# A retention layer with an MLP on one core: decay in q and v alone, states copied, g folded into w1, x normalized ahead of the first product

## The chip, the core and the metric

The program runs on one core of a Trainium2 chip. Five engines work beside each other, each in its own order: TensorE (PE, matmul; its weight loads are shown as PEld), VectorE (DVE), ScalarE (ACT), GpSimd (POOL) and SyncE (SP). They wait for one another by semaphores. Sixteen DMA engines move data; SP, ACT and POOL put transfers on queues. TensorE writes into eight PSUM banks of 128 x 512 float32; the other engines read the results from there. The metric is device time in microseconds.

## What is computed

For four batches and eight heads a state of 64 x 64 decays by a head's factor at each of 768 positions and takes up k times v; q reads it. The heads side by side give x of 512 columns, which goes through a normalization, two matrices with a relu between them, and a residual.

```python
gamma = 1.0 - 2.0 ** (-5.0 - np.arange(H))
for t in range(S):
    state = gamma * state + einsum('bhd,bhe->bhde', k[:, :, t], v[:, :, t])
    y[:, :, t] = scale * einsum('bhd,bhde->bhe', q[:, :, t], state)
x = y.transpose(0, 2, 1, 3).reshape(B, S, 512)
xn = (x - mean(x)) / sqrt(var(x) + 1e-6) * g_ln
out = x + maximum(xn @ w_ch1, 0) @ w_ch2          # 512 x 2048, 2048 x 512
```

Inputs and output are float32.

## The kernel before

**Tiles.** The 768 positions of a batch are six chunks of 128, so there are 24 tiles of 128 positions. `TILES` numbers the four chunks 0 first (tiles 0 to 3), then chunks 1 to 5 of batch 0 (4 to 8), of batch 1 (9 to 13) and so on. Matrices are bfloat16 on the chip, sums float32.

**A tile's attention.** q, k and v are loaded (tokens `q`, `k`, `v`; POOL issues them, and the transfer turns float32 into bfloat16). For tiles 0 to 6 (`T0` = 7) TensorE transposes q and k into PSUM (`tq`, `tk`); for later ones a DMA transpose on SP's queue does it (`tr`). `eq` multiplies the transposed q by a decay that grows from the start of the chunk, `qsc`. `vis` makes the scores of k and q, and from tile 7 on also the product of q with the state; from tile 8 on it does so for two tiles at once. `am` multiplies the scores by `mask`, which holds the causal triangle and the inverse decay of the key's position. `py` multiplies them with v. The same v times an inverse decay counted from the start of the sequence (`vg`, POOL) goes with k into the running sum of a batch, which one PSUM bank holds (`pd`, bank PD), and `pb` reads that sum into a bfloat16 state, multiplied by the decay of the chunk's start (`gch`): two VectorE instructions, one per half of the partitions, since a state holds pairs of heads and only the diagonal blocks are written; the rest was set to zero at the start.

**A tile's MLP.** `bn` takes mean and variance, `xn` subtracts the mean and multiplies by g, `xc` copies y into `x_all` for the residual. Up to tile 9 (`S0` = 10) the division by the standard deviation comes last, in the addition `ad`, since relu lets a positive factor pass; from tile 10 on ScalarE does it behind `xn` (`sr`, `rt`, `xg`), on a float32 copy. `tx` and `ex` transpose x for the first product, tiles 0 to 7 on TensorE, later ones by DMA. The first product (`m`) goes by groups of one, two or four tiles: a piece fills one bank (16, 8 or 4 matmuls of 128, 256 or 512 columns), and a relu (`r`, mostly ScalarE) empties it. The second product goes tile by tile (`z`, 16 matmuls of 512 columns), but from tile 10 on two tiles together with seven products in place of eight (`s` 1 to 7, Strassen's scheme in Winograd's form): four sums of weight blocks are made once (`tm`), four differences of blocks of relu output per pair (`sa`, VectorE), and `o` adds the products and x together. `st` stores a tile from ScalarE's queue.

**Weights.** w1 comes in four column pieces of 512 (`W0` to `W3`), w2 in four row pieces (`Z0` to `Z3`), all on POOL's queue. `gb` spreads g over the partitions by a float32 matmul. `warm` is a matmul on zeros.

**The order** is written out by hand: `ORDER` lists tokens, and each engine runs its own in that order. `m0_4//X1` is a piece of the first product into bank X1, `r0_4/A` its relu on ScalarE, `/D` means VectorE, `/S` SP, `/P` POOL. Most banks have a fixed part: X0 to X3 scores and the first product, Y0 and Y1 y, M the second product, PD the running sum. POOL's loads stand in its own order, and before a load that overwrites a buffer it waits with a one-element copy (`gate`).

## Time and profile before

| | us |
|---|---|
| three runs | 208.21, 1157.15, 210.58 |
| median | 210.58 |
| span of the profiled execution | 205.7 |

The page gives of the profiled execution its span, from the first to the last instruction, and no other time. The fastest of the three runs lies 2.5 above that span; one run was disturbed. A row such as "busy us" counts an engine's time in instructions; a matmul's own duration is longer than its distance to the next, because matmuls overlap. The chain of waits follows the work back from the last instruction. The granted TensorE clock was 0.997 over the span.

The start in order of time, by the chain: TensorE, ScalarE and VectorE have first data from 4.2 us on, the first product with w1 starts at 14.4 us. POOL issues its last load at 132.7 us; the last DMA transpose is issued at 163.5 us.

### The profile page before, as it was taken

The numbers are of one execution on the slowest core, as the hardware profiler recorded it, in microseconds if no ns is written. First come the engines' busy times: TensorE is split into PE (matmuls) and PEld (weight loads), VectorE is DVE, ScalarE is ACT, GpSimd is POOL, SyncE is SP. The second block draws the span as 40 slices with busy tenths as digits, with TensorE's granted clock in tenths as the row PEclk, the third lists the DMA queues.
The fourth block names the chain that finished last, engine by engine and source line by source line (L and its number), as shares of the span: only waits on it lengthen the run. The fifth ranks groups of instructions, "written<-read, shape, count | busy, mean of one in ns | idle before, by whom it ended". The sixth has DMA issues, their size and how long they took to land.

```text
span 205.7 us, 5388 instructions
## 1 busy us (share of the span) xinstructions
PE 198.7 (97%) x2183; PEld 147.5 (72%) x2183; DVE 156.4 (76%) x365; ACT 87.1 (42%) x191; POOL 96.5 (47%) x145
## 2 busy tenths in 40 slices
PE   7998999999999999999998999999999999999993
PEld 2568999898546568577784988987465876458882
DVE  7687889678249979979899999999868674026972
ACT  6375653650400504646263173590766504562000
POOL 8995694694498597492598077900000000000000
PEclk9999999999999999999999999999999999999998
DMA  8999999999999999999999999997010313111025
GB/s 127 166 183 178 162 191 168 174 182 153 160 110 181 140 123 137 180 92 175 171 175 154 136 247 169 164 160 138 3 51 0 81 26 149 58 51 51 0 101 208
DMA packets 109948, 27.13 MB, mean 132 GB/s; under 512 B 102626, under 2 KB 106978, under 8 KB 109923
## 3 DMA queue, kind: packets, MB, share of 16 engines
q0 software_dynamic: 77024, 13.37, 86.5%
q1 hardware_dynamic: 28242, 6.85, 25.4%
q10 hardware_dynamic: 4656, 6.56, 10.1%
q8 instruction: 17, 0.28, 0.6%
q14 instruction: 9, 0.07, 0.1%
HBM read 27.30 MB, written 6.29 MB: 163 GB/s over the span
## 4 chain that ended last, share of the span: by engine, by line
PE 81%; DVE 7%; DMA 5%; POOL 3%; issue 2%; ACT 1%; POOLq 0%; ACTq 0%
PE X L529 35%; PE M L547 12%; PE M L606 10%; PE Y L606 5%; DMA w<-in_moe_w_ch_dram 5%; PE Y L547 3%; PE X L606 3%; PE PD L606 3%; PE X L404 2%; PE Y L432 2%; DVE sum L595 2%; PE PD L474 2%; DVE asb L417 1%; POOL early L346 1%; POOL k L346 1%
## 5 line engine op out<-in xcount | busy, mean ns | idle before, releaser
L529 PE MATMUL X<-xnt,w 128*128 128x128 bf16 (+2 forms) x880 | 89.6, 255 | 0.5 <-DMA w<-in_moe_w_ch_dram 0.5
L529 PEld LDWEIGHTS <-w 128*128 128x128 bf16 x896 | 66.3, 98 | 19.4 <-DMA w<-in_moe_w_ch_dram 0.7
L540 ACT ACTIVATE h<-X 128x512 bf16<-128x512 f32 x85 | 48.5, 601 | 50.9 <-PE X L529 46.3
L417 DVE TENSOR_TENSOR asb<-X,mask 128x512 bf16<-128x512 f32 x48 | 30.5, 683 | 3.3 <-PE X L404 3.1
L547 PE MATMUL M<-w,h 128*128 128x512 bf16 x128 | 30.6, 379 | 0.0
L456 ACT CAST x_all<-Y 128x256 bf16<-128x256 f32 (+1 forms) x39 | 14.4, 408 | 28.7 <-DVE bns L440 13.1
L547 PEld LDWEIGHTS <-h 128*128 128x128 bf16 x160 | 14.9, 98 | 14.8
L466 POOL TENSOR_TENSOR vg<-v,vsc 128x512 bf16<-128x512 bf16 x19 | 20.1, 1058 | 9.9 <-DMA v<-in_v_dram 9.9
L606 PEld LDWEIGHTS <-h 128*128 128x128 bf16 x224 | 21.7, 98 | 3.5 <-issue 0.3
L346 POOL DMA_DIRECT2D v<-in_v_dram x23 | 20.8, 907 | 3.0 <-DMA w<-in_moe_w_ch_dram 2.5
L440 DVE BATCH_NORM_STATS2 bns<-Y 128x6 f32<-128x256 f32 (+1 forms) x39 | 16.1, 450 | 5.2 <-PE Y L432 4.6
L606 PEld LDWEIGHTS <-sum 128*128 128x128 bf16 x168 | 16.3, 98 | 2.8 <-issue 0.3
L484 DVE TENSOR_TENSOR state<-PD,gch 64x256 bf16<-64x256 f32 x40 | 16.6, 414 | 0.3
L346 POOL DMA_DIRECT2D qk<-in_q_dram x17 | 15.2, 895 | 1.3 <-issue 0.7
L346 POOL DMA_DIRECT2D qk<-in_k_dram x17 | 15.2, 898 | 0.9 <-issue 0.8
L620 DVE TENSOR_TENSOR osb<-M,x_all 128x256 f32<-128x256 f32 (+1 forms) x12 | 6.1, 505 | 10.5 <-PE M L606 10.4
L595 DVE TENSOR_TENSOR sum<-h,sum 128x1024 bf16<-128x1024 bf16 x14 | 10.6, 756 | 0.2
L395 DVE TENSOR_TENSOR trq<-tr,qsc 128x512 bf16<-128x512 bf16 x17 | 7.6, 454 | 3.3 <-DMA tr<-qk 3.2
L626 PE MATMUL PD<-zeros 128*128 128x512 bf16 (+1 forms) x33 | 8.9, 404 | 1.2 <-DVE zeros L259 1.2
L375 POOL COPY scrap<-qk 1x1 bf16<-1x1 bf16 x28 | 5.8, 208 | 8.1 <-DMA qk<-in_k_dram 7.2
L432 PEld LDWEIGHTS <-asb 128*128 128x128 bf16 x192 | 8.0, 98 | 2.1 <-DVE asb L417 0.4
L552 DVE SCALAR_TENSOR_TENSOR osb<-M,rstd,x_all 128x512 f32<-128x512 f32 x8 | 6.0, 750 | 3.5 <-PE M L547 3.5
(115 smaller groups left out, 256.6 us busy)
## 6 DMA issues: line engine op xcount, KB each, us to landing
out_dram<-osb ACTq DMA_DIRECT2D x23, 256.0 KB, 2.5
w<-in_moe_w_ch_dram POOLq DMA_DIRECT2D x8, 512.0 KB, 8.7
v<-in_v_dram POOLq DMA_DIRECT2D x23, 128.0 KB, 7.1
qk<-in_k_dram POOLq DMA_DIRECT2D x17, 128.0 KB, 6.0
qk<-in_q_dram POOLq DMA_DIRECT2D x17, 128.0 KB, 6.6
early<-in_q_dram POOLq DMA_DIRECT2D x6, 128.0 KB, 7.5
k<-in_k_dram POOLq DMA_DIRECT2D x3, 128.0 KB, 7.6
early<-in_k_dram POOLq DMA_DIRECT2D x3, 128.0 KB, 8.5
```

The costliest lines, as they stand in the source:

```text
L346: nc.gpsimd.dma_start(out=dst, in_=tok[kind][TILES[t]])
L417: nc.vector.tensor_tensor(out=slot(asb, t)[:, :, par, :], in0=bank(("pa", t, par)).rearrange("p (i t) -> p i t", t=P), in1=mask.rearrange( ...
L432: nc.tensor.matmul(dst, lhsT=slot(asb, t)[:, h // 2, h % 2, :], rhs=v_of(t)[:, h, :], start=(not late and n == H and h == 0), stop=(h >= H ...
L440: nc.vector.bn_stats(out=bns[:, t, i, :], in_=x)
L456: nc.scalar.copy(out=dst, in_=src)
L466: nc.gpsimd.tensor_tensor(out=slot(vgs, chunk(t)), in0=v_of(t), in1=vsc[:, c, :].unsqueeze(2).to_broadcast([P, H, D]), op=ALU.mult)
L484: nc.vector.tensor_tensor(out=slot(state, chunk(t) - 1)[o, :, o], in0=pd[o, :, o], in1=gch[o, c - 1, :].unsqueeze(2).to_broadcast([D, NPAI ...
L529: nc.tensor.matmul(bank(("mm", g, ho))[:, j * n * P:(j + 1) * n * P], lhsT=w1[:, ko, (ho + j) * P:(ho + j + 1) * P], rhs=x[:, x0:x0 + n, k ...
L540: nc.scalar.activation(out=dst, in_=src, func=AF.Relu)
L547: nc.tensor.matmul(bank(("m2", t)), lhsT=slot(h1, t // 4)[:, ho, t % 4 * P:(t % 4 + 1) * P], rhs=w2[:, ho, :], start=(ho == 0), stop=(ho = ...
L595: {"P": nc.gpsimd, "": nc.vector}[eng].tensor_tensor(out=out, in0=in0, in1=in1, op=ALU.subtract)
L606: nc.tensor.matmul(product(t, i), lhsT=left(t, i)[:, ho, :], rhs=right[i][:, ho, :], start=(ho == 0 and i in (1, 2)), stop=(ho == HK - 1), ...
```

## The change

Decay. q is multiplied by a decay counted from the start of the sequence, so there is a table `qsc` for each chunk (six; one made by ScalarE, one by VectorE, four by POOL), and v by its inverse for all tiles (`vg`, now also the right side of `py`). The mask is then the plain triangle `cm`, and a state needs no factor: `pb` is one copy of the whole bank, 17 of 20 on ScalarE.

```diff
-        nc.vector.tensor_tensor(out=slot(trq, t), in0=x, in1=qsc, op=ALU.mult)
+        nc.vector.tensor_tensor(out=slot(trq, t), in0=x, in1=qscs[TILES[t][1]], op=ALU.mult)
...
-            in1=mask.rearrange("p (i a) t -> p a i t", a=2)[:, par], op=ALU.mult)
+            in1=cm.unsqueeze(1).to_broadcast([P, NPAIR, P]), op=ALU.mult)
...
-        for o in (slice(0, D), slice(D, P)):
-            nc.vector.tensor_tensor(
-                out=slot(state, chunk(t) - 1)[o, :, o], in0=pd[o, :, o],
-                in1=gch[o, c - 1, :].unsqueeze(2).to_broadcast([D, NPAIR, D]), op=ALU.mult)
+        evacuate(eng, slot(state, chunk(t) - 1), BANK["PD"].rearrange("p (i t) -> p i t", t=P))
...
+    @on("qs")
+    def _(eng, c):
+        if c == 0:
+            nc.scalar.activation(out=qscs[c], in_=arg, func=AF.Exp, bias=ln8, scale=1.0)
+            return
+        e = nc.vector if eng == "D" else nc.gpsimd
+        e.tensor_tensor(out=qscs[c], in0=qsf, in1=gch[:, c - 1, :].unsqueeze(2).to_broadcast([P, NPAIR, P]),
+                        op=ALU.mult)
```

Tiles 4 to 6 take the state in `vis` by halves of the partitions too, in place of the whole-pair product ahead of `py`.

g. It comes as four columns of 128 (`gc`, SP), and VectorE multiplies each piece of w1 by it after it lands and before its first use (`wg`, four instructions a piece). The matmul that spread g is gone.

```diff
+    @on("wg")
+    def _(eng, j):
+        s = slice(j * DM, (j + 1) * DM)
+        for ko in range(KO):
+            nc.vector.tensor_scalar(out=w1[:, ko, s], in0=w1[:, ko, s], scalar1=gcol[:, ko:ko + 1], scalar2=None,
+                                    op0=ALU.mult)
```

Normalization. For every tile the reciprocal of the standard deviation (`sr` on ScalarE, `rt` on VectorE) and the shift (`sh`, VectorE) are made first, and `xn` then does all of it in one instruction on either engine; `xg` and the float32 copies are gone, and `ad` only adds.

```diff
+        nc.vector.scalar_tensor_tensor(out=shift[:, t:t + 1], in0=mv[:, t, 0:1], scalar=-1.0,
+                                       in1=rstd[:, t:t + 1], op0=ALU.mult, op1=ALU.mult)
...
-        dst, src, g = y_parts(t, half, slot(xns if t < S0 else xhat, t))
-        nc.vector.scalar_tensor_tensor(out=dst, in0=src, scalar=mv[:, t, 0:1], in1=g,
-                                       op0=ALU.subtract, op1=ALU.mult)
+        dst, src = y_parts(t, half, slot(xns, t))
+        if eng == "A":
+            nc.scalar.activation(out=dst, in_=src, func=AF.Identity, bias=shift[:, t:t + 1],
+                                 scale=rstd[:, t:t + 1])
+        else:
+            nc.vector.tensor_scalar(out=dst, in0=src, scalar1=mv[:, t, 0:1], scalar2=rstd[:, t:t + 1],
+                                    op0=ALU.subtract, op1=ALU.mult)
```

So the pair of tiles 8 and 9 can go through the seven products as well (eight pairs, not seven; `z` for tiles 0 to 7).

Order. `y_of` takes its two banks by the table too, so that any bank may hold anything but the running sum. The `gate` copies, the early read of w1 (`touch`) and the zeroing of states are gone. Attention begins with tiles 0, 2, 4, 1. Of 96 relus ScalarE keeps 57 (89 before); of 32 `sa` POOL takes 16; of 44 `xn` ScalarE takes 25; of 25 stores SP takes 13. Two of its lines:

```diff
-vis0//X1,X2 gb//X3 W1 am0b vg0/ am0a gl v2 warm3_2 tq1//Y1 py0//M tk1//Y0 eq1 ek1/A k3 bn0 sqt
+vis1//X1,X3 k3/P q3/P am1b/D tq4//Y1 eq4/D rt0/D vg4/P py2//Y0 pb4/A bn2/D ba2/D sh0/D W2/P ek4/A
```

POOL's first loads before; `early`, `k_`, `v_` are buffers of single tiles, `w_92` is w1, so that its pieces are rows five and eight.

```order
L346 DMA early<-in_v_dram 128x8x64
L346 DMA k_99<-in_k_dram 128x8x64
L346 DMA early<-in_q_dram 128x8x64
L346 DMA v_102<-in_v_dram 128x8x64
L365 DMA w_92<-in_moe_w_ch_dram 128x4x512
L346 DMA k_100<-in_k_dram 128x8x64
L346 DMA early<-in_q_dram 128x8x64
L365 DMA w_92<-in_moe_w_ch_dram 128x4x512
L466 TENSOR_TENSOR vg_132<-early,vsc 128x512
```

The same start of POOL after the change (`w_95` is w1):

```order
L348 DMA k_102<-in_k_dram 128x8x64
L348 DMA v_107<-in_v_dram 128x8x64
L348 DMA early<-in_q_dram 128x8x64
L348 DMA v_109<-in_v_dram 128x8x64
L367 DMA w_95<-in_moe_w_ch_dram 128x4x512
L348 DMA v_106<-in_v_dram 128x8x64
L480 TENSOR_TENSOR vg_133<-v_107,vsc 128x512
L348 DMA k_104<-in_k_dram 128x8x64
L348 DMA early<-in_q_dram 128x8x64
L480 TENSOR_TENSOR vg_135<-v_109,vsc 128x512
L367 DMA w_95<-in_moe_w_ch_dram 128x4x512
```

Five more tile loads stand ahead of what is shown, so the first piece of w1 is POOL's tenth load, not its fifth, and between it and the next come three tile loads and two products of v with the decay.

VectorE around its first work for tile 0's and 1's MLP before (`bns` statistics, `asb` masked scores, `trq` scaled q):

```order
L440 BN_STATS bns<-M 128x6
L441 BN_AGGR mv<-bns 128x2
L450 SCALAR_TENSOR_TENSOR xn_137<-M,mv,gb 128x512
L417 TENSOR_TENSOR asb_136<-X_64,mask 128x4x128
L417 TENSOR_TENSOR asb_136<-X_61,mask 128x4x128
L440 BN_STATS bns<-M 128x6
```

And after, where VectorE scales the first piece of w1 (`w_95`):

```order
L421 TENSOR_TENSOR asb_139<-Y_66,cm 128x4x128
L421 TENSOR_TENSOR asb_139<-X_64,cm 128x4x128
L451 RECIPROCAL rstd<-rstd 128x1
L455 SCALAR_TENSOR_TENSOR shift<-mv,rstd 128x1
L373 TENSOR_SCALAR w_95<-w_95,gcol 128x512 x4
L439 BN_STATS bns<-X_63 128x6
L439 BN_STATS bns<-M 128x6
L443 BN_AGGR mv<-bns 128x2
L421 TENSOR_TENSOR asb_140<-X_62,cm 128x4x128
```

The four scalings stand between the shift of tile 2 and the statistics of tile 4, and a masked score of tile 1 (the last row) comes behind them.

The third place is VectorE at the pair of tiles 14 and 15. Before, their masked scores (four `asb`) are followed by a state and statistics:

```order
L417 TENSOR_TENSOR asb_135<-X_62,mask 128x4x128
L417 TENSOR_TENSOR asb_135<-X_61,mask 128x4x128
L417 TENSOR_TENSOR asb_136<-X_64,mask 128x4x128
L417 TENSOR_TENSOR asb_136<-X_63,mask 128x4x128
L484 TENSOR_TENSOR state_95<-PD,gch 64x4x64 x2
L440 BN_STATS bns<-Y_65 128x6
```

After:

```order
L421 TENSOR_TENSOR asb_139<-M,cm 128x4x128
L421 TENSOR_TENSOR asb_139<-X_64,cm 128x4x128
L421 TENSOR_TENSOR asb_140<-X_63,cm 128x4x128
L421 TENSOR_TENSOR asb_140<-Y_66,cm 128x4x128
L399 TENSOR_TENSOR trq_131<-tr_122,qsc_82 128x512
L399 TENSOR_TENSOR trq_128<-tr_125,qsc_84 128x512
L439 BN_STATS bns<-X_61 128x6
```

The scaled q of tiles 19 and 16 (`trq`), which read what DMA transposes bring (`tr`), now stand between the masks and the statistics.

More of the change, by code (lines that the diff above doesn't have):

```diff
@@ L32 @@
 ORDER = """
-hk0b/A hk0a/S iota small pos hq0b/A hq0a/S v0 grow table touch k1 consts idn arg lmul cm q1 vsc mask
-qsc v1 hkc0/A gch hqc0a/D zero W0 warm8_1 tk0//Y0 hqc0b/A k2 ek0/A warm1_1 tq0//Y1 eq0 q2 warm1_3
-vis0//X1,X2 gb//X3 W1 am0b vg0/ am0a gl v2 warm3_2 tq1//Y1 py0//M tk1//Y0 eq1 ek1/A k3 bn0 sqt
-warm3_1 vis1//X3,X0 q3 xn0 v3 am1a xc0 warm2_3 tx0//Y0 am1b ex0/A W2 warm3_0 py1//M warm1_0 tk2//Y0
-pd0 k4 bn1 ek2/A tq2//Y1 q4 m0_0//X3 xn1 eq2 r0_0/D vis2//X1,X2 tx1//Y0 am2a am2b m0_4//X0 v4 xc1
@@ L166 @@
     rstd = sb.tile([P, NT], FP32, name="rstd")
-    touch = sb.tile([P, KO, 16], FP32, name="touch")
+    shift = sb.tile([P, NT], FP32, name="shift")
     w1 = sb.tile([P, KO, DH], BF16, name="w1")
@@ L179 @@
     q0 = [early_h[:, 4 + i] for i in range(4)]
-    v0 = [early_h[:, 11]] + [sb.tile([P, H, D], BF16, name=f"v0{i}") for i in range(1, B)]
     trk = [early_t[:, 8 + i] for i in range(3)]
@@ L185 @@
     trq = slots("trq", [P, NPAIR, P], BF16)
+    vg0 = [early_h[:, 11]] + [sb.tile([P, H, D], BF16, name=f"vg0{i}") for i in range(1, B)]
     vgs = slots("vg", [P, H, D], BF16)
@@ L308, in _ @@
                                 op0=ALU.is_ge)
-    @on("mask")
+    @on("gc")
     def _(eng):
-        nc.vector.tensor_tensor(
-            out=mask, in0=vsc[:, 0, :].unsqueeze(2).to_broadcast([P, H, P]),
-            in1=cm.unsqueeze(1).to_broadcast([P, H, P]), op=ALU.mult)
-    @on("gch")
-    def _(eng):
-        for c in range(1, C):
-            nc.scalar.activation(out=gch[:, c - 1], in_=lgq, func=AF.Exp, bias=0.0,
-                                 scale=float(P * c))
-    @on("zero")
-    def _(eng):
-        for x in state:
-            nc.vector.memset(x, 0.0)
-    @on("grow")
-    def _(eng):
-        nc.sync.dma_start(out=grow[0:1, :], in_=moe_g_ln.rearrange("(o n) -> o n", o=1))
-    @on("touch")
-    def _(eng):
-        nc.sync.dma_start(out=touch, in_=w1_v[:, :, 0:16])
-    @on("gb")
-    def _(eng):
-        nc.tensor.matmul(bank(("mm", "g")), lhsT=ones, rhs=grow[0:1, :], start=True, stop=True)
-    @on("gl")
-    def _(eng):
-        nc.scalar.copy(out=gb, in_=bank(("mm", "g")))
+        dma(eng).dma_start(out=gcol, in_=moe_g_ln.rearrange("(ko p) -> p ko", p=P))
     @on("k", "q", "v")
@@ L406, in _ @@
         for t in ts:
-            for i in range(NPAIR if t >= T0 else 0):
+            for i in range(NPAIR if TILES[t][1] else 0):
                 for par in range(2):
@@ L671, in parse @@
-        if kind == "z":
-            t, part = map(int, arg.split("_"))
-            if where:
-                at(("m2", t))
-            return EMIT[kind], (t, part)
-        if kind == "warm":
-            return EMIT[kind], tuple(map(int, arg.split("_")))
-        return EMIT[kind], (int(arg),) if arg else ()
+        kind, arg = re.fullmatch(r"([a-zA-Z]+?)(\d.*)?", name).groups(default="")
+        keys = []
+        if kind in ("hk", "hq", "hkc", "hqc"):
+            n, half = re.fullmatch(r"(\d+)([ab]?)", arg).groups()
+            args, kind = (letter[half], kind[1], int(n)), "hc" if kind.endswith("c") else "ha"
+        elif kind in ("k", "q", "v"):
+            args = (kind, int(arg))
+        elif kind in ("tk", "tq"):
+            args = (kind[1], int(arg))
+            keys = [("tp", *args)]
+        elif kind in ("xn", "xc", "am", "st"):
+            n, half = re.fullmatch(r"(\d+)([ab]?)", arg).groups()
+            args = (int(n), letter[half])
+        else:
+            args = tuple(map(int, arg.split("_"))) if arg else ()
+            if kind == "tx":
+                keys = [("tp", "x", *args)]
+            elif kind == "vis":
+                ts = visit[args[0]]
+                keys = [("pa", t, par) for t in ts for par in range(2)] + [("y", ts[0], par) for par in range(2)]
+            elif kind == "py":
+                keys = [("y", *args)]
+            elif kind == "m":
+                keys = [("mm", *args)]
+            elif kind == "s":
+                keys = [("sm" if args[1] == 1 else "sb", args[0])]
+            elif kind == "z":
+                keys = [("m2", args[0])]
```

310 lines of the change are left out of this document (133 added, 177 removed).

## The prediction

> **What bounds the kernel now.** I read the page from the top: the share of busy time, then the chain that ended last, then the busy time by stage, then the places where TensorE waits.
>
> ```profile
> span 205.7 us, 5388 instructions
> PE 198.7 (97%) x2183; PEld 147.5 (72%) x2183; DVE 156.4 (76%) x365; ACT 87.1 (42%) x191; POOL 96.5 (47%) x145
> q0 software_dynamic: 77024, 13.37, 86.5%
> PE 81%; DVE 7%; DMA 5%; POOL 3%; issue 2%; ACT 1%; POOLq 0%; ACTq 0%
> ```
>
> TensorE is busy for 97% of the span and carries 81% of the chain. It is the bound. The loads that POOL issues (queue q0) fill 86.5% of sixteen DMA engines' span, so the feed is the second tight resource. VectorE, at 76% over the whole span, is nearly full in one stage:
>
> ```profile
> core 0: us, PE busy (x) PEld busy (x) DVE busy (x) ACT busy (x) POOL busy (x), PEclk, DMA share, GB/s
> 5.00:15.00 10.00, 9.56 (x101) 5.93 (x100) 7.36 (x16) 5.36 (x12) 9.77 (x13) 1.00 1.86 175
> 15.00:25.00 10.00, 9.06 (x168) 8.51 (x166) 8.17 (x17) 5.46 (x11) 6.48 (x8) 1.00 2.11 169
> 100.00:140.00 40.00, 39.03 (x435) 33.02 (x432) 38.75 (x88) 20.50 (x46) 24.70 (x36) 1.00 1.63 172
> 140.00:206.00 66.00, 62.22 (x518) 43.13 (x516) 39.81 (x89) 23.10 (x48) 0.00 (x0) 0.99 0.22 69
> ```
>
> From 100 to 140 us VectorE works 38.75 of 40 us, yet TensorE still works 39.03: the vector backlog costs TensorE about 1 us there. After 140 us nothing but TensorE is tight. Busy time in the first 15 us misleads, because much of it is matmuls on zeros. What counts there is when real work can run:
>
> ```profile
> 14.42 1.06 PE L529 MATMUL X<-xnt,w 128*128 128x128 bf16 x16
> 16.79 1.07 PE L529 MATMUL X<-xnt,w 128*128 128x128 bf16 x16 [0.54 <-DMA w<-in_moe_w_ch_dram]
> 20.91 0.40 PE L404 MATMUL X<-trq,early 64*128 64x128 bf16 x8 [0.36 <-DVE trq L395]
> ```
>
> The first w1 product starts at 14.42, the second stands until the second piece of w1 lands, and from 20.91 on TensorE is never held for long. The chain gives the price of each piece of TensorE work as the distance from one start to the next:
>
> ```profile
> 7.47 9.27 DMA w<-in_moe_w_ch_dram
> 18.09 0.89 PE X L529 x16
> 33.47 0.22 PE Y L426 x4
> 73.67 0.55 PE X L404 x16
> 74.22 0.23 PE Y L410 x16
> 82.47 1.73 PE M L547 x8
> 163.95 0.87 PE M L606 x8
> 202.25 0.42 DVE osb L620
> ```
>
> So a group of w1 products is 0.89, four z products (1.73 / 2) are 0.86, eight Strassen products 0.87, a set of four 128-column products 0.22, a single tile's scores 0.28 (half of 0.55), its state products 0.12. Counting the order table with these (and 0.5 for the product that spreads g), the kernel before holds 186.2 us of TensorE work. Before 20.91 it has done 8.3 of it: 12 sets at 0.22, three scores at 0.28, three y at 0.23, g, four w1 groups at 0.89. The start therefore loses 20.91 - 8.3 = 12.6 us. From 20.91 to 202.25 there are 181.3 us for 177.9 of work: 3.4 us of small waits. Then 205.7 - 202.25 = 3.4 us to the end: last add, store, landing.
>
> **The change, part by part.** *TensorE's work.* One more tile pair (8, 9) goes through the seven products: 8 z pieces fewer (-6.9) and 7 s pieces more (+6.1). Tiles 4 to 6 drop the whole-pair state product (-3 x 0.22) for the split one (+3 x 0.12). The product for g goes (-0.5). Together -1.6: 184.6 us. The 26 zero matmuls that remain (33 before) stand ahead of the first product and only fill waiting time.
>
> *The start.* POOL issues its loads in order, and they land in order. Four of them give the pace, each by issue plus time to landing:
>
> ```profile
> L346 POOL DMA_DIRECT2D v<-in_v_dram x1: 913/913/913, 4.1 to 4.1; - x1
> DMA to landing us min/median/max: 5.0/5.0/5.0
> L365 POOL DMA_DIRECT2D w<-in_moe_w_ch_dram x1: 802/802/802, 5.0 to 5.0; - x1
> DMA to landing us min/median/max: 7.5/7.5/7.5
> L346 POOL DMA_DIRECT2D v<-in_v_dram x1: 928/928/928, 11.9 to 11.9; - x1
> DMA to landing us min/median/max: 8.2/8.2/8.2
> L365 POOL DMA_DIRECT2D w<-in_moe_w_ch_dram x1: 814/814/814, 12.8 to 12.8; - x1
> DMA to landing us min/median/max: 9.9/9.9/9.9
> ```
>
> The fourth tile load lands at 9.1, the first w1 piece at 12.5 (3.4 later), the second at 7.47 + 9.27 = 16.7, four tile loads after it at 20.1 (0.84 each), the third w1 piece at 22.7 (2.6 later). In the new POOL order W0 stands behind nine tile loads, not four: 9.1 + 5 x 0.84 + 2.6 to 3.4 = 15.9 to 16.7. Then come three tile loads and W2: 21.0 to 22.6 (23.5, if W2, issued at about 16 behind 14 loads at 0.9 and two vg at 1.06, needs W0's 7.5). Each w1 piece is now scaled by g on VectorE ahead of its first use: four TENSOR_SCALAR of 128x512 bf16, a form the trace lacks. It lies between the 0.27 of idn (a quarter of the elements, f32) and the 0.45 of trq (two inputs), both below; I take 0.3, nearer idn since it too has one input: 1.2 us a piece. Those that wait for W0 and W2 also hold all of VectorE behind them: the bn of tile 4, then am of tile 1, on which py1 waits.
>
> With W0 alone TensorE can do everything up to m2_8, the first group that reads W2: 16 sets at 0.22, five scores, one state, four y and three w1 groups, 8.7 us. So m2_8 starts at 21.9 + 1.2 + 0.1 = 23.2 (22.2 to 24.8), and the start loses 23.2 - 8.7 = 14.5, 1.9 more than before. Afterwards W1 (+0.84 + 2.6, at 25.4) and W3 (28) come ahead of their use: five w1 groups and a y, 4.7 us, stand between m2_8 and the first that reads W1.
>
> *Side engines.* Rows:
>
> ```profile
> L484 DVE TENSOR_TENSOR state<-PD,gch 64x256 bf16<-64x256 f32 x40 | 16.6, 414 | 0.3
> L571 ACT ACTIVATE xn<-grow,rstd 128x512 bf16<-128x512 f32 x7 | 5.0, 721 | 7.1 <-DVE rstd L567 4.2 <-DVE grow L450 1.8 <-ACT h L540 0.9
> L395 DVE TENSOR_TENSOR trq<-tr,qsc 128x512 bf16<-128x512 bf16 x17 | 7.6, 454 | 3.3 <-DMA tr<-qk 3.2
> L302 DVE TENSOR_SCALAR idn<-fidx,pos 128x128 bf16<-128x128 f32 x1 | 0.3, 273 | 0.0
> L466 POOL TENSOR_TENSOR vg<-v,vsc 128x512 bf16<-128x512 bf16 x19 | 20.1, 1058 | 9.9 <-DMA v<-in_v_dram 9.9
> ```
>
> The state's decay leaves VectorE (-16.6); 17 plain copies go to ScalarE, which was busy 42% and loses the 14 xg (-10.1) and 32 relus. VectorE takes those relus and the w1 scaling (16 x 0.3 = 4.8), and gives 25 of 44 normalizations to ScalarE and 12 subtractions net to POOL. No sum of this moves the end: ScalarE keeps over half its time free, VectorE gets slightly lighter. What VectorE's full stage cost TensorE, about 1 us, is the most that relief there returns.
>
> *Costed at nothing.* The load of g by columns is SP's third DMA, where grow's stood, and has until W0 lands. The four decay tables that POOL makes (about 1.1 each, like vg) stand ahead of later loads in POOL's queue; the loads already issued keep the DMA engines at work meanwhile, and if they ran dry each would cost its 1.1. Of 25 stores 13 move to SP's queue, behind transposes; they delay an output buffer, of which three pairs exist, and only those at the end lie on the path, where SP has nothing else left. Three shorter steps (aggregate, reciprocal, shift) stand ahead of x's normalization instead of behind it, covered by the 2 to 10 us of work between y and its transpose in the order table.
>
> *POOL against VectorE.* POOL gains 16 subtractions of 128x1024. No row shows one on POOL; vg, half as long, takes 1.06, so I take 2.1, with VectorE's 0.68 as the other end. What matters more is this:
>
> ```profile
> 108.14 2.46 DVE L595 TENSOR_TENSOR sum<-h 128x1024 bf16<-128x1024 bf16 x1
> 109.01 1.03 POOL L466 TENSOR_TENSOR vg<-v,vsc 128x512 bf16<-128x512 bf16 x1
> 117.13 0.68 DVE L595 TENSOR_TENSOR h<-h 128x1024 bf16<-128x1024 bf16 x1
> ```
>
> A VectorE subtraction of 0.68 took 2.46 while POOL ran a vg, and ended 0.56 after it: VectorE stood behind POOL. POOL's elementwise work rises from 20 x 1.06 = 21 to 22 x 1.06 + 4 x 1.1 + 16 x 2.1 = 61 us, so such meetings cost more. Between none and 1.8 us for each of the 16 subtractions left to VectorE (29 us) I take 1 us on TensorE: VectorE has a quarter of its time free, and in the last chain the POOL subtractions have 2.6 us (three groups at 0.87) of cover against 2.1. The Trainium skill (SBUF — State Buffer, Terms) calls this pair of ports an exclusive lock held for the whole instruction; the 2.46 row agrees. By that rule every such meeting would cost VectorE up to POOL's full 2.1 us, which is the slower rival below.
>
> *The end* is the same chain of add, store and landing: 3.4.
>
> **Sum.** 14.5 lost at the start + 184.6 work + 3.4 small waits + 1.0 meetings + 3.4 end = 206.9 us of span, against 205.7: +0.6%. The page gives no time for that execution itself beside its span. The fastest run, 208.21, lies 2.5 above the span, the median, 210.58, 4.9 above. I add the middle, 3.7: 210.6, the median of before.
>
> **Rivals.** *Faster.* If w1 lands as early as before, the start keeps its 12.6, and if VectorE's relief ends the small waits down to 1 us: 12.6 + 184.6 + 1 + 3.4 = 201.6, so 205.3 (-2.5%). For it: fewer waits of POOL on copied gates, and the 32 KB of touch less. Against it: the landing pace of 0.84 in the rows above. Chance 0.22.
>
> *Slower: POOL holds VectorE.* Behind each held subtraction wait relus and score masks that free PSUM banks, on which TensorE's next groups wait. If a third of 16 x 1.8 us reaches TensorE, 8.6 more than my 1.0: 219; it decides (over 2%) from 5 us, that is from a sixth. For it: the 2.46 row. Against it: after 140 us VectorE works 39.81 of 66. I give 0.20, with 216 as its middle.
>
> *Slower: transposes late.* The new order puts the scaling of q of tiles 17 and 19 directly behind their DMA transposes.
>
> ```profile
> tr<-qk SPq DMA_TRANSPOSE x17, 5.8
> ```
>
> If SP gets to them only when VectorE does, each holds VectorE, and the score masks and relus behind, for up to 5.8 us; one full hold, less about 1 that TensorE covers with groups at hand, gives 215. Against it: the loads are issued over 10 us of work ahead, so SP can go early. Chance 0.10.
>
> *Cold array.* Start-to-start, a 512-column product on zeros takes 0.41 in the first row, and a set of four transposes 0.42 at 5.79 (to the next start at 6.21) but 0.22 in the later chain:
>
> ```profile
> 1.19 3.70 PE L626 MATMUL PD<-zeros 128*128 128x512 bf16 x9 [1.19 <-DVE zeros L259]
> 5.79 0.63 PE L381 MATMUL Y<-idn,early 128*128 128x128 bf16 x4
> 6.21 0.49 PE L626 MATMUL PD<-zeros 128*128 128x512 bf16 x1
> ```
>
> TensorE begins at half speed. With fewer fillers between 7 and 17 us it may fall back; then three w1 groups cost 2.7 more, of which the wait for W2 hides about 1: 212.3. The Trainium skill (TensorE: Matmul & The Clock Gate, What's actually happening) has the array halve its clock after an idle window of about 3.4 us. By that rule real work at most 3 us apart avoids it. Chance 0.06.
>
> **How the numbers follow.** The forecast has 0.42, the cold array 0.06, faster 0.22, slower 0.30. Taking 2%, about what a measurement of this kernel can tell from no change: faster 0.22, same 0.48, slower 0.30. The likeliest case's own range is 208.4 to 213.4 (the W2 bounds, -1.0 and +1.6, and 2.5 to 4.9 around the span). The 8-in-10 range reaches into both others: 204.5 to 217.
>
> **What would show it.** Right: the first w1 product near 17.5, the first that reads the third piece near 23, 61 us of elementwise POOL time, VectorE subtractions stretched beside POOL's, last matmul near 203.5. Wrong: a first product before 15.5, or gaps on TensorE above 6 us in all after 25 us, or the DMA pace below 0.7 us a tile.

## The result, and the profile after

The changed kernel takes 230.61 us (median of 4 runs, 229.04 to 232.82) against 209.40 for the kernel before beside it: 1.105 times as long, 95% interval 1.094 to 1.117. Forecast were 210.6 us and a range of 204.5 to 217. The profiled execution took 229.16 us with a span of 227.4, where the forecast had a span of 206.9.

From the page of the changed kernel, the span, TensorE's share, the loads that POOL issues, and the chain that ended last by engine:

```profile
span 227.4 us, 5423 instructions
PE 203.0 (89%) x2210; PEld 152.4 (67%) x2210; DVE 170.6 (75%) x378; ACT 84.7 (37%) x186; POOL 130.9 (58%) x126
q0 software_dynamic: 77024, 13.37, 86.2%
PE 37%; DMA 25%; POOL 18%; DVE 12%; issue 5%; SPq 1%; ACT 0%; POOLq 0%; DVEq 0%
```

TensorE's share fell from 97 to 89%, and its part of the chain from 81 to 37%: DMA, POOL and VectorE now end waits that TensorE pays for. The same stretches as before, with the columns of the table in the prediction (each engine's busy time and instructions, then the granted clock):

```profile
5.00:15.00 10.00, 7.99 (x110) 5.21 (x108) 8.35 (x21) 5.45 (x13) 8.91 (x12) 1.00 2.38 163
15.00:25.00 10.00, 7.10 (x70) 6.37 (x71) 9.45 (x22) 6.05 (x14) 9.26 (x11) 0.52 1.58 168
100.00:140.00 40.00, 32.69 (x367) 27.33 (x366) 31.71 (x62) 12.56 (x29) 23.20 (x20) 0.96 1.21 122
140.00:206.00 66.00, 62.84 (x564) 43.37 (x561) 51.09 (x112) 24.70 (x58) 26.41 (x16) 1.00 0.34 61
```

Two things stand out. From 15 to 25 us the granted clock is 0.52, where it was 1.00. And from 100 to 140 us TensorE works 32.69 us of 40, where it worked 39.03.

To place the loss, "lost time" is used below: the start of a TensorE instruction less the price of all real products ahead of it (0.216, 0.109, 0.056 and 0.029 us for 512, 256, 128 and 64 columns, the distance between starts in these traces at full clock; half of it for a product that reads 64 partitions, since these run in pairs, and nothing for the one that spread g). Before the change 13.4 us are lost at 8 us of work, 13.9 at 20, 15.3 at 85, 16.6 at 100 and 17.7 at the end. After it: 18.5, 21.5, 24.0, 33.3 and 40.7. Against the kernel before, 7.6 us more are lost by 20 us of work (41 us after the start of the span), 1.1 from there to 85, 8.0 from 85 to 100 (109 to 133 us after the start), and 6.3 from there to the end. Times below are medians of all runs and ratios go by undisturbed runs alone, but the profiled executions of three kernels (fill_noscale, norm, no_scale_norm) were disturbed ones, so of their times only the first 42 us are read.

The start, on TensorE's timeline of the changed kernel (start, length, instruction, count, idle time ahead of it and what ended it):

```profile
15.76 0.61 PE L503 MATMUL Y<-idn,xn 128*128 128x128 bf16 x4 [1.36 <-ACT xn L466]
...
17.72 0.61 PE L503 MATMUL Y<-idn,xn 128*128 128x128 bf16 x4 [0.93 <-ACT xn L466]
18.12 0.42 PE L519 MATMUL X<-xnt,w 128*128 128x128 bf16 x2
19.75 1.82 PE L519 MATMUL X<-xnt,w 128*128 128x128 bf16 x14 [1.21 <-DVE w L373]
...
26.99 1.06 PE L519 MATMUL X<-xnt,w 128*128 128x128 bf16 x16
```

TensorE waits for x's normalization twice, then for the scaled w1; and the fourteen products take 1.82 us where sixteen take 1.06 later. The last row is the first group that reads the third piece of w1. And the scaling itself, first all sixteen as a group (count, shortest, median and longest in ns, first and last start), then on VectorE's timeline:

```profile
L373 DVE TENSOR_SCALAR w<-w,gcol x16: 332/700/1840, 16.2 to 37.7; 128x512 bf16<-128x512 bf16 x16
```

```profile
16.22 3.73 DVE L373 TENSOR_SCALAR w<-w,gcol 128x512 bf16<-128x512 bf16 x4
...
24.91 1.93 DVE L373 TENSOR_SCALAR w<-w,gcol 128x512 bf16<-128x512 bf16 x4
...
29.94 3.27 DVE L373 TENSOR_SCALAR w<-w,gcol 128x512 bf16<-128x512 bf16 x4
...
34.74 3.32 DVE L373 TENSOR_SCALAR w<-w,gcol 128x512 bf16<-128x512 bf16 x4
```

A piece takes 1.9 to 3.7 us on VectorE, not 1.2. The shortest, 0.33, is near the 0.3 assumed; the median is twice that. Six of the sixteen took 0.33 to 0.35 us. The other ten took 0.66 to 1.84, and each of these ended 0.09 to 0.25 us after the end of a POOL instruction (a load's issue or a product of v), which stand one behind the other there.

The middle, where most is lost, on TensorE's timeline:

```profile
117.29 1.04 PE L582 MATMUL Y<-w,h 128*128 128x256 bf16 x8
121.52 1.87 PE L519 MATMUL X<-xnt,w 128*128 128x256 bf16 x8 [3.19 <-DMA xnt<-xn]
123.18 1.72 PE L519 MATMUL M<-xnt,w 128*128 128x256 bf16 x8
124.74 1.04 PE L519 MATMUL X<-xnt,w 128*128 128x256 bf16 x8
...
131.54 1.03 PE L519 MATMUL X<-xnt,w 128*128 128x256 bf16 x8 [2.04 <-DVE xn L469]
```

The wait at 118 us is for a DMA transpose of x, and the two groups behind it take 1.87 and 1.72 us in place of 1.04. That transpose was issued at 112.8 us, behind two transposes of q and k on SP's queue, and took 8.6 us to land; before the change those issued from 86 to 99 us landed in 4.0 to 6.0. The rows after, then before:

```profile
L512 SPq DMA_TRANSPOSE xnt<-xn x1: 1661/1661/1661, 112.8 to 112.8; - x1
...
DMA to landing us min/median/max: 8.6/8.6/8.6
```

```profile
L504 SPq DMA_TRANSPOSE xnt<-xn x4: 1191/1207/2307, 86.4 to 99.0; - x4
...
DMA to landing us min/median/max: 4.0/4.4/6.0
```

The wait at 129 us has another source, seen on VectorE's timeline and then on POOL's:

```profile
127.48 3.10 DVE L455 SCALAR_TENSOR_TENSOR shift<-mv,rstd 128x1 f32<-128x1 f32 x1
130.50 0.53 DVE L469 TENSOR_SCALAR xn<-Y,mv,rstd 128x256 bf16<-128x256 f32 x1
```

```profile
127.52 0.88 POOL L348 DMA_DIRECT2D qk<-in_k_dram  x1
128.41 2.14 POOL L571 TENSOR_TENSOR h<-h 128x1024 bf16<-128x1024 bf16 x1
```

An operation on one number per partition, 0.16 us in the median, stood on VectorE for 3.10 us and ended when POOL's subtraction did. The first 0.9 us of it lie beside POOL's issue of a load, not beside the subtraction.

### The profile page after: what moved, and what is told of

Same layout as the page of the kernel before. It is cut to its first block, busy times and chain, and to the rows that moved or that the text cites. A ratio compares the mean times of both kernels' runs of the same rounds, so it can differ in the third digit from the quotient of the medians.

```text
span 227.4 us, 5423 instructions
## 1 busy us (share of the span) xinstructions
PE 203.0 (89%) x2210; PEld 152.4 (67%) x2210; DVE 170.6 (75%) x378; ACT 84.7 (37%) x186; POOL 130.9 (58%) x126
## 4 chain that ended last, share of the span: by engine, by line
PE 37%; DMA 25%; POOL 18%; DVE 12%; issue 5%; SPq 1%; ACT 0%; POOLq 0%; DVEq 0%
DMA v<-in_v_dram 16%; PE X L519 9%; PE X L582 6%; DMA xnt<-xn 5%; POOL qk L348 5%; PE Y L582 4%; DMA qk<-in_k_dram 4%; PE PD L519 4%; POOL vg L480 3%; DVE sum L571 3%; POOL v L348 3%; PE Y L519 3%; POOL early L348 3%; PE M L519 3%; DVE h L532 2%
## 5 line engine op out<-in xcount | busy, mean ns | idle before, releaser
L519 PE MATMUL X<-xnt,w 128*128 128x128 bf16 (+2 forms) x520 | 55.2, 258 | 8.9 <-DMA xnt<-xn 3.8
L571 POOL TENSOR_TENSOR sum<-h,sum 128x1024 bf16<-128x1024 bf16 x9 | 19.4, 2160 | 49.6 <-DVE sum L571 35.8
L530 ACT ACTIVATE h<-X 128x512 bf16<-128x512 f32 x33 | 19.5, 600 | 35.9 <-PE X L519 35.7
L537 PE MATMUL X<-w,h 128*128 128x512 bf16 x96 | 22.8, 379 | 0.0
L519 PE MATMUL Y<-xnt,w 128*128 128x128 bf16 (+2 forms) x220 | 22.6, 254 | 0.1
L582 PEld LDWEIGHTS <-sum 128*128 128x128 bf16 x192 | 18.5, 98 | 5.8 <-issue 2.8
L571 POOL TENSOR_TENSOR h<-h 128x1024 bf16<-128x1024 bf16 x6 | 13.3, 2210 | 14.6 <-DVE sum L571 14.6
L421 DVE TENSOR_TENSOR asb<-X,cm 128x512 bf16<-128x512 f32 x29 | 19.0, 679 | 3.5 <-PE X L408 2.5
L348 POOL DMA_DIRECT2D qk<-in_k_dram x17 | 15.3, 905 | 7.9 <-PE PD L487 7.8
L532 DVE TENSOR_SCALAR h<-X 128x512 bf16<-128x512 f32 x20 | 13.5, 677 | 6.3 <-PE X L519 6.2
L348 POOL DMA_DIRECT2D qk<-in_q_dram x17 | 15.4, 912 | 0.0
L519 PE MATMUL M<-xnt,w 128*128 128x256 bf16 (+2 forms) x120 | 14.3, 268 | 0.9 <-issue 0.9
L475 ACT CAST x_all<-X 128x256 bf16<-128x256 f32 (+1 forms) x23 | 8.8, 398 | 14.5 <-DVE bns L439 9.6
L582 PE MATMUL X<-w,h 128*128 128x256 bf16 x88 | 11.2, 272 | 2.7 <-DVE osb L596 2.7
```

The source lines that it names most:

```text
L348: nc.gpsimd.dma_start(out=dst, in_=tok[kind][TILES[t]])
L421: nc.vector.tensor_tensor(out=slot(asb, t)[:, :, par, :], in0=bank(("pa", t, par)).rearrange("p (i t) -> p i t", t=P), in1=cm.unsqueeze(1) ...
L475: nc.scalar.copy(out=dst, in_=src)
L519: nc.tensor.matmul(bank(("mm", g, ho))[:, j * n * P:(j + 1) * n * P], lhsT=w1[:, ko, (ho + j) * P:(ho + j + 1) * P], rhs=x[:, x0:x0 + n, k ...
L530: nc.scalar.activation(out=dst, in_=src, func=AF.Relu)
L532: nc.vector.tensor_scalar_max(out=dst, in0=src, scalar1=0.0)
```

## The experiments

All edits are made to the changed kernel, and each time is compared with runs of the kernel before the change (about 208.7 us) on the same chip. Three of the pieces are small helpers: `fillN` issues N products of zeros of 512 columns that are added to the state's bank and so leave it as it is,

```diff
+    @on("fill")
+    def _(eng, n):
+        for _ in range(n):
+            nc.tensor.matmul(BANK["PD"], lhsT=zeros[:, 0:P], rhs=zeros, start=False, stop=False,
+                             skip_group_check=True)
```

`sa…/P` becomes `sa…/D` (a subtraction for the seven products on VectorE), and `tx`, `ex/A` replace `ex/S` (x transposed by TensorE and copied by ScalarE, not by a DMA transpose).

### The start: cold array or scaling

**Zeros in the waits of the start** (`fill`):

```diff
+fill7 tx0//Y1 ... +fill5 tx2//Y1 ... +fill8 m0_0//X0 +fill2 py1//X1 ... +fill2 tx4//M
```

> The changed kernel with 24 more products of zeros, each 512 columns and added to the state's bank (which they leave as it is), in the five waits that TensorE has between 14 and 23 us. Theory A, the scaling of w1 on VectorE sets the start: the clock stays full, but the third piece of w1 is scaled no earlier than now (done at 26.8), so the first group that reads it starts at most 1 us earlier and the kernel gains 0 to 1.5 us of about 229. Theory B, the cold array sets it: groups that took 1.8 us take 0.9, three of them and five short sets between 15 and 26 us are done 3 to 4 us earlier, the kernel gains 3 to 4 us.

**No scaling of w1** (`noscale`): the four `wg` are taken out, so the result lacks g.

> The changed kernel without the sixteen scalings of w1 by g (so g is missing from the result). Theory A, the scaling sets the start: the groups of w1 products wait for the landings alone (15.7, 23.0, 26.4, 28.9), the waits on scaled w1 between 18 and 38 us (4 us on TensorE in all) go, and VectorE's other work comes 2 to 4 us earlier: gain 3 to 5 us of about 229. Theory B, the cold array sets it: the granted clock stays at half between 15 and 25 us, so most of what is won is lost again by products at half speed: gain 0 to 2 us.

**Both** (`fill_noscale`).

> Both edits of the two runs before: 24 more products of zeros between 14 and 23 us and no scaling of w1 by g (g is missing from the result). If scaling and cold array each cover the other (either alone gives little), both together give 5 to 7 us of about 229 and the loss at 20 us of work done falls from 21.5 to about 15. If they add up, the gain is the sum of the two single ones. If the feed of w1 (W2 at 23.0) sets the start in the end, the gain is no more than the larger single one.

| kernel | time, us | ratio (95%) | lost at 8, at 20 us of work |
|---|---|---|---|
| changed | 230.61 | 1.105 (1.094–1.117) | 18.5, 21.5 |
| fill | 223.66 | 1.072 (1.062–1.082) | 17.5, 22.0 |
| noscale | 230.55 | 1.108 (1.100–1.116) | 15.5, 17.1 |
| fill_noscale | 227.19 | 1.086 (1.076–1.097) | 16.5, 16.9 |

In the start itself theory A holds and theory B falls. With zeros the clock is full, as the stretches of that kernel show,

```profile
15.00:20.00 5.00, 4.71 (x44) 2.32 (x40) 4.41 (x14) 2.94 (x6) 3.76 (x4) 1.00 1.83 171
20.00:25.00 5.00, 4.95 (x73) 4.14 (x73) 3.83 (x11) 3.59 (x9) 4.98 (x7) 1.00 1.38 178
```

and still the loss at 20 us of work is 22.0: TensorE only arrives sooner at w1 that is not scaled yet. Without the scaling it is 17.1, and zeros besides change that little (16.9). One execution is no finer than some 1.4 us here: five kernels with the very same start (changed, sub_vector, loads_first, x_tensor, fill_middle) begin the scores of tile 6 between 42.05 and 43.45 us. But the times run the other way round: the kernel with the better start is no faster, and the one with the same start is 7 us faster. Both theories of the end-to-end time failed, so the start could not be what decides. Of the three readings of fill_noscale the last is left: it gains no more than fill alone. Landmarks of the same work show where it turns (start of the scores of a tile or pair, us):

| kernel | tile 6 | 8, 9 | 12, 13 | 16, 17 | span |
|---|---|---|---|---|---|
| changed | 43.30 | 69.75 | 99.06 | 134.47 | 227.4 |
| noscale | 38.88 | 65.81 | 98.75 | 135.34 | 228.7 |
| fill | 43.80 | 70.97 | 99.78 | 130.34 | 221.8 |

Noscale loses its 4.4 us again by 99 us, most of it at 84 us, where it waits for a DMA transpose of x and sixteen products behind the wait take 3.27 us, at half the clock:

```profile
85.71 3.27 PE L517 MATMUL X<-xnt,w 128*128 128x256 bf16 x16 [2.10 <-DMA xnt<-xn]
```

Fill is 0.7 us behind at 99 us, and wins 4.9 between there and 130 us.

### The middle: POOL, the queues, the clock

**All subtractions on VectorE** (`sub_vector`).

> The changed kernel with all its subtractions for the seven products on VectorE, those of POOL too (15 of 2.16 us there become 15 of 0.68 here, 10 us). Theory P, POOL's subtractions cost the middle and the end (loads held behind them, VectorE held beside them): the waits of TensorE between 104 and 139 us (8 us lost there) and most of those after 144 us (6 us) go, gain 8 to 12 us of about 229. Rival V, VectorE is the bound from 100 to 140 us: the 10 us more on it cost TensorE what the waits of POOL cost, gain below 3 us or a loss.

Measured: 223.25 us, ratio 1.070 (1.063 to 1.078). That is some 7 us below the changed kernel, a little less than theory P wanted and far from rival V. A subtraction that stood beside POOL's on VectorE was stretched, as the group in the changed kernel and then that in this one show (count, busy time, mean ns of one):

```profile
L571 DVE TENSOR_TENSOR sum<-h,sum 128x1024 bf16<-128x1024 bf16 x7 | 8.5, 1221 | 0.3
```

```profile
L569 DVE TENSOR_TENSOR sum<-h,sum 128x1024 bf16<-128x1024 bf16 x16 | 11.0, 689 | 0.3
```

From the scores of 16, 17 on the changed kernel needs 92.9 us and this one 90.2, and from those of 18, 19 on, where only the last pairs are left, 75.6 and 74.3.

**Loads ahead of POOL's first subtraction** (`loads_first`).

```diff
-sa8_3/P
+q19/P k21/P v18/P k20/P q22/P sa8_3/P
```

> The changed kernel with five loads (q19, k21, v18, k20, q22) moved in POOL's order ahead of the first POOL subtraction, behind which they now stand idle from 90 to 99.5 us. All subtractions stay on POOL. Theory Q, the held loads are what POOL's subtractions cost: loads, transposes of q and k, and the transpose of x behind them on SP's queue come earlier, the waits of TensorE at 118 us (3.4) and 129 us (2.2) shrink, and the gain is 4 to 6 us of about 229, near the 6 us that subtractions on VectorE gave. Theory L, it is VectorE held beside POOL's subtractions: gain 0 to 1 us.

Measured: 231.11 us, 1.106 (1.099 to 1.112): no gain, theory Q falls as stated. The wait at 118 us is gone, but a longer one stands at 111. On TensorE's, VectorE's and POOL's timelines of this kernel:

```profile
116.05 1.31 PE L580 MATMUL X<-early,sum 128*128 128x256 bf16 x8 [4.73 <-DVE osb L594]
```

```profile
109.45 5.61 DVE L453 SCALAR_TENSOR_TENSOR shift<-mv,rstd 128x1 f32<-128x1 f32 x1
114.98 0.41 DVE L397 TENSOR_TENSOR trq<-tr,qsc 128x512 bf16<-128x512 bf16 x1
```

```profile
109.48 2.14 POOL L569 TENSOR_TENSOR h<-h 128x1024 bf16<-128x1024 bf16 x1
111.56 2.12 POOL L569 TENSOR_TENSOR sum<-h,sum 128x1024 bf16<-128x1024 bf16 x1
113.63 1.04 POOL L478 TENSOR_TENSOR vg<-v,vsc 128x512 bf16<-128x512 bf16 x1
```

With no load between them, three POOL operations ran one behind the other, and a VectorE operation of 0.16 us (median) stood until 0.4 us after the end of the third: 5.61 us. This is the clearest sight of theory L's mechanism. The Trainium skill (SBUF — State Buffer, Terms) has VectorE and GpSimd take one pair of ports as an exclusive lock for whole instructions, with the loser fully blocked; these rows agree. Here the loser did not get in between back-to-back POOL operations, but that is no rule: in the changed kernel the same operation at 158.48 us stood 1.74 us beside one subtraction and ended with it, though a product of v followed at once.

**x of tiles 12 and 13 transposed on TensorE** (`x_tensor`).

```diff
-ex12/S
+tx12//X2 ex12/A
-ex13/S
+tx13//X2 ex13/A
```

> The changed kernel with x of tiles 12 and 13 transposed on TensorE and copied by ScalarE (8 short products, 0.45 us in all) in place of two DMA transposes on SP's queue, on the later of which TensorE waits 3.4 us at 118 us. Theory S, that transpose on the queue is the bound there and the wait drops the clock behind it: the wait goes, the clock stays full from 120 to 125 us (1.7 us), gain 3 to 5 us of about 229. Rival D, VectorE is late there by itself, since it stands at 118.7 to 120.3 for a transpose of k and q: the wait passes on to the products behind it, gain below 2 us.

Measured: 225.15 us, 1.081 (1.071 to 1.091), and no wait above 1.23 us between 100 and 134. Theory S holds: from the scores of 14, 15 to those of 16, 17 this kernel needs 18.0 us, the changed one 22.0.

**Zeros in the wait at 118 us only** (`fill_middle`).

```diff
-m10_4//X3
+fill10 m10_4//X3
```

> The changed kernel with ten products of zeros (512 columns, 2.2 us at full clock, added to the state's bank) ahead of the group that waits 3.4 us at 118 us for a DMA transpose of x; nothing else is touched, so that group can start no earlier. Theory C, that wait lets the clock fall and the fall is what separates the kernels of 229 to 231 us (waits of 3.4 to 4.9 us there) from those of 223 to 225 (waits of at most 2.5): the two groups behind it take 1.04 each in place of 1.87 and 1.72, the late wait at 129 us shifts, gain 3 to 6 us of about 229. Rival S, only the length of the wait counts: gain below 1 us.

Measured: 225.21 us, 1.082 (1.074 to 1.091). The group still waits for its transpose, on TensorE's timeline,

```profile
117.34 2.10 PE L606 MATMUL PD<-zeros 128*128 128x512 bf16 x9
120.62 1.03 PE L517 MATMUL X<-xnt,w 128*128 128x256 bf16 x8 [1.18 <-DMA xnt<-xn]
121.49 1.04 PE L517 MATMUL M<-xnt,w 128*128 128x256 bf16 x8
```

but the products behind it run at full rate, and the wait of 2.04 us at 129 us is gone too, since VectorE and POOL meet elsewhere. Theory C holds, but not all of the 5 us is the zeros': the scores of 14, 15, ahead of which the two kernels are the same, already start at 111.44, not 112.49. From there to the scores of 16, 17 it is 18.5 us against 22.0, so ten useless products win 3.5 us: 1.7 of slow clock and the 2.0 at 129 us, less 0.2. The clock differs in all runs, not only in the profiled ones: over the span it was 0.956 to 0.970 in the changed kernel, 0.977 to 0.985 here and 0.992 to 1.000 in fill. Read together, the runs line up by the wait and the clock behind it:

| kernel | longest TensorE wait, 100 to 130 us | clock in the 5 us that hold what follows | time, us |
|---|---|---|---|
| changed | 3.19 | 0.66 | 230.61 |
| noscale | 3.60 | 0.52 | 230.55 |
| loads_first | 4.73 | 0.67 | 231.11 |
| fill_sub (below) | 2.31 | 0.66 | 225.25 |
| fill | 2.03 | 1.00 | 223.66 |
| sub_vector | 1.52 | 1.00 | 223.25 |
| fill_middle | 1.23 | 1.00 | 225.21 |
| x_tensor | 1.23 | 1.00 | 225.15 |

The table sorts kernels by this one wait; it doesn't rank all times, since fill_sub has the slow clock and still 225.25. Fill's gain does not come from the start, where its zeros stand: it reaches the middle 0.7 us later, while the group behind the transpose starts at 121.07, not 121.52, so its wait is 2.03 us and the clock stays. That is luck, not what the zeros were put in for.

### Do the gains add up?

**Zeros at the start and subtractions on VectorE** (`fill_sub`), and **x of tiles 8 to 13 on TensorE besides** (`fill_sub_x`).

> The 24 more products of zeros and all subtractions on VectorE, both in one kernel (each alone gave 6 us: 223.7 and 223.3 of about 229). If they cure separate losses, the time is 216 to 218. If both only keep the middle from running into the long waits at 118 and 129 us, the gain is counted twice and the time is 221 to 223.

> The kernel with more products of zeros and all subtractions on VectorE, and x of tiles 8 to 13 transposed on TensorE too (24 short products, 1.3 us). Theory S, DMA transposes of x on SP's queue hold the stretch from 60 to 125 us: what the start wins is then kept, and the time is 3 to 5 us below the kernel without it. Rival: loads of q and k set that stretch, the time stays within 1.5 us of it or rises by the 1.3.

Measured: 225.25 us (1.079, 1.069 to 1.089) and 223.22 (1.067, 1.058 to 1.076). They do not add up: each alone had already removed the same wait. The first has a wait of 2.31 us at 102.7 with a cold array (the clock at half) behind it. The second has no wait above 0.8 us from 100 to 130, but its clock falls at 40 us,

```profile
40.00:44.00 4.00, 4.00 (x46) 3.93 (x44) 1.21 (x3) 1.09 (x2) 4.00 (x5) 0.57 1.24 205
```

behind the waits for scaled w1, and the scores of tile 6 start at 46.25, 3 us later than in the changed kernel.

**The same without scaling** (`no_scale_all`), **with half the scaling on ScalarE** (`split_all`), **and with POOL's loads held back** (`no_scale_spaced`).

```diff
-v9/P ... vg9/P ... vg8/P
+v9/P vg9/P vg8/P
```

> More products of zeros at the start, all subtractions on VectorE, x of tiles 8 to 13 transposed on TensorE, and no scaling of w1 (g is missing from the result): the kernel that gave 223.2 us, without the scaling. Without scaling alone the start was 4.4 us earlier at 41 us, but all of it was lost again by 99 us. Theory X, it was the DMA transposes of x that took it back (2.3 us of wait at 83 us and the clock behind it): then 4 to 5 us are kept here, 217 to 219. Rival T, transposes of q and k, which take 9 us from issue to landing between 55 and 85 us, take it back whatever x does: a wait of 2 to 4 us stands near 65 to 77 us and the time stays at 221 or more.

> The same as the kernel that gave 223.2 us (zeros at the start, subtractions on VectorE, x of tiles 8 to 13 transposed on TensorE), with half of each w1 piece scaled by ScalarE beside VectorE (two of 128x512 each): everything is computed. If the scaling on VectorE holds the start, half of its 4.4 us comes back there and the waits between 31 and 38 us (3 us) halve: 219 to 221. If ScalarE's copies ahead of TensorE's transposes are late behind its scalings, no gain or a loss of 1 us.

> The kernel without scaling of this group (g is missing), with the two gated copies of v of tiles 8 and 9 moved forward in POOL's order, behind the load of v9 that they wait for: POOL's next fourteen loads then start at about 59 us in place of 52, and the transposes of q and k of tiles 8 to 11 do not stand behind them in the DMA engines. Theory T: those transposes land in 5 to 6 us in place of 9, waits between 60 and 80 us go, gain 1 to 4 us on the kernel without this move. Rival F, the engines only run dry: later loads come 4 to 7 us later, pairs from 12 on wait for them, loss of 1 to 5 us.

| kernel | time, us | ratio (95%) | tile 6 | 8, 9 | 12, 13 | 16, 17 | span |
|---|---|---|---|---|---|---|---|
| no_scale_all | 218.87 | 1.050 (1.044–1.057) | 38.99 | 67.38 | 97.16 | 125.85 | 216.1 |
| split_all | 220.45 | 1.058 (1.051–1.065) | 42.00 | 68.47 | 98.32 | 127.57 | 217.9 |
| no_scale_spaced | 220.21 | 1.058 (1.051–1.066) | 39.68 | 66.12 | 98.64 | 127.19 | 217.6 |

Split_all comes out inside its range; no version that computes everything is faster, and it is still 5.8% slower than the kernel before. No_scale_all lies in theory X's range, but not all is kept: it is 3.0 us ahead of split_all at tile 6 and 1.1 at 8, 9. What takes the rest is rival T's mechanism, on VectorE's and TensorE's timelines of no_scale_all:

```profile
65.71 0.42 DVE L398 TENSOR_TENSOR trq<-tr,qsc 128x512 bf16<-128x512 bf16 x1 [2.56 <-DMA tr<-qk]
```

```profile
67.38 0.40 PE L407 MATMUL X<-trq,tr 64*128 64x128 bf16 x8 [1.87 <-DVE osb L541]
```

VectorE stands for a DMA transpose of q and k, and the add behind it, which TensorE needs, stands too. No_scale_spaced shows why that transpose is late. The two transposes issued at 54 to 56 us, in no_scale_all and then with the loads held back:

```profile
L392 SPq DMA_TRANSPOSE tr<-qk x2: 1232/2130/3027, 54.1 to 55.5; - x2
...
DMA to landing us min/median/max: 7.2/8.7/10.1
```

```profile
L392 SPq DMA_TRANSPOSE tr<-qk x2: 1232/1260/1287, 54.5 to 55.8; - x2
...
DMA to landing us min/median/max: 3.2/3.4/3.5
```

They are slow behind POOL's loads, and with the loads held back 8, 9 start 1.3 us sooner than in no_scale_all: theory T is right on the spot. But 12, 13 start 1.5 us later, and the median is 1.3 us longer, with intervals that overlap. A loss of that size is rival F's, but the wait behind it is not one for a late load:

```profile
94.00 1.02 PE L536 MATMUL M<-w,h 128*128 128x512 bf16 x4 [1.93 <-DVE h L531]
```

TensorE waits for a relu on VectorE. Ahead of that relu VectorE's shift took 1.38 us and a sum of weight blocks 2.06, where no_scale_all has 0.16 and 1.22, and POOL was making products of v at 89.08 and 91.03: VectorE and POOL meet once more.

### What is left of the start

**The first two tiles' normalization moved forward**, alone (`norm`), without scaling (`no_scale_norm`), in the complete kernel (`split_norm`): aggregate, root, reciprocal and shift ahead of the masks and copies they stood behind.

```diff
-bn0/D ... ba0/D sr0/A ... am2a/D ... rt0/D ... sh0/D ... sr2/A rt2/D ... xn0/A xc0/A sh2/D
+bn0/D ba0/D ... sr0/A ... am2a/D rt0/D sh0/D ... ek4/A xn0/A sr2/A ... am4a/D rt2/D sh2/D
```

> The changed kernel with the short steps of the first two tiles' normalization (aggregate, root, reciprocal, shift) moved on VectorE and ScalarE ahead of a score mask or a copy each, behind which they now stand; nothing is added or left out. Theory N, x's normalization ahead of its transpose sets the first w1 product: it starts at 16 to 17 us in place of 18.1, the waits of 1.5 and 1.1 us at 14 and 16.5 us shrink. By itself little of that reaches the end, since the scaling of w1 holds the same products: gain 0 to 2 us of about 229, or 4 to 6 if the wait at 118 us comes out short of the one that lets the clock fall. Rival: the landing of w1 at 15.7 sets it, and the first product moves by less than 0.5 us.

> The kernel of 218.9 us (zeros at the start, subtractions on VectorE, x of tiles 8 to 13 transposed on TensorE, no scaling, so g is missing from the result), with the normalization of the first two tiles moved forward as in the run before, and fewer zeros. Theory N: what the start still loses without scaling (16.6 us at 8 us of work done, against 13.4 in the kernel before the change) is the normalization: 14 to 14.5 are lost, and the time falls by 1 to 3 us if the stretch from 55 to 100 us lets it through. Rival F: it is the feed (third piece of w1 at 23.0), and the loss at 8 us of work done stays above 16.

> The kernel of 220.5 us that computes everything (w1 scaled by VectorE and ScalarE in halves, zeros at the start, subtractions on VectorE, x of tiles 8 to 13 transposed on TensorE), with the normalization of the first two tiles moved forward. Theory N: 1 to 2 us less, 218.5 to 219.5, still slower than the kernel before the change. Rival F: within 0.7 us of 220.5.

Measured: 232.73 us (1.108, 1.091 to 1.125), 222.24 (1.064, 1.050 to 1.077) and 220.41 (1.058, 1.047 to 1.068). None is faster than the kernel without the move. In norm the first w1 product starts at 18.9 us, not 16 to 17: on TensorE's timeline a transpose of x now waits for a score mask,

```profile
16.49 0.59 PE L501 MATMUL Y<-idn,xn 128*128 128x128 bf16 x4 [0.88 <-DVE asb L419]
```

so theory N falls as stated: what VectorE does sooner for x it does later for the masks. Without scaling 15.8 us are lost at 20 us of work, against 17.1 with the old order and no zeros and 17.2 with the old order and 24 zeros (here 12): the move gives some 1.3 us at the start, in one execution each. Where they go afterwards is not shown. That the two us then left against the kernel before (13.9) are the feed of w1 is likely, not shown.

## Why the prediction was wrong

The sum had 14.5 us lost at the start, 3.4 of small waits and 1.0 of meetings, 18.9 in all; 40.7 were lost. For the kernel before, the sum's prices gave 16.0 (12.6 + 3.4) where the prices used here give 17.7, so the even comparison is 2.9 us more than before, forecast, against 23.0. Step by step:

- **Right: TensorE's work, the feed.** By the same prices TensorE has 1.1 us less work than before, as forecast (1.6, with 0.5 for the product that spread g, which these prices leave out). The third piece of w1 landed at 23.0 us (forecast 21.0 to 22.6, at most 23.5).
- **"Each w1 piece is now scaled ... I take 0.3": mis-sized.** A scaling took 0.70 in the median, a piece 1.9 to 3.7 us. The first group that reads the third piece started at 26.99, not 23.2, and the later pieces cost waits of their own. Without scaling 4.4 us less are lost at 20 us of work, the larger part of the 5.7 by which the start was missed (7.6 more lost than before, forecast 1.9).
- **"Three shorter steps ... covered by the 2 to 10 us of work": failed.** There was no such work at 14 us: TensorE waited 1.36 and 0.93 for the normalized x. Moved forward, they only pass the wait on to a score mask.
- **"3.4 small waits", carried over from the kernel before: the step that failed most.** After the start 19.2 us were lost, not 4.4 (15.4 more than before, forecast 1.0). The cover that the old order kept over DMA transposes was gone: the one at 112.8 us took 8.6 to land. The prediction looked for late transposes of q at tiles 17 and 19 holding VectorE (chance 0.10); it was x's transpose behind them on SP's queue that TensorE waited for. With x of those two tiles on TensorE about 5 us come back, 4.0 of them between the scores of 14, 15 and 16, 17.
- **The cold array: right mechanism, wrong place, chance 0.06 too low.** The clock fell at 15 us as that rival said, but there it cost little that the scaling did not cover: with zeros 22.0 us are lost, not 21.5. At 121 us it cost the most: zeros in that wait win 3.5 us. "Real work at most 3 us apart avoids it" was wrong twice: the clock fell at 15 us with no wait above 1.36, and behind a wait of 2.31.
- **POOL against VectorE: half right.** POOL's subtraction took the 2.1 us forecast. The "1 us on TensorE" is about what it costs from 18, 19 on (75.6 against 74.3 us). In the middle it is more: VectorE's 3.10 us at 127.5 stood in TensorE's path. What the sum watched was subtractions held beside subtractions; what was held there, and 5.61 us in loads_first, was an operation on one number per partition. All of POOL's subtractions together cost 7 us, of which the clock's share comes back by other edits as well, so the terms can't be told apart as a sum.
- **Reading across.** Most of these faults share one: the sum priced each wait by itself. Here one wait of 3.2 us drags a slow clock behind it, and a start that comes 4.4 us earlier runs into the next late transpose.

What stays open: 10 us between the best variant without scaling (218.87) and the kernel before. Three of them are lost at the start (17.2 against 13.9 at 20 us of work), 1.3 are its 24 transposes on TensorE, 1.9 the wait at 65 us; the rest was not taken apart. Nor were the 6.3 us that the changed kernel loses behind 133 us, beyond the 2.7 that come back from the scores of 16, 17 on with all subtractions on VectorE. That stores were moved to SP's queue was not tried by itself, nor was scaling with POOL silent: that POOL makes the scaling slow rests on where the ten slow ones end, and on no experiment.
